# Last spectra reloaded in two parts and by tile pairs, four buffers for the first transform's results, four gate products in wide PSUM pairs, and a new written order

## The chip, the cores and the metric

The kernel runs on one core of a Trainium2 chip. Its time is device microseconds (us) of one execution. Before the change it is 236.85 us, the median of 3 runs, which lie between 234.69 and 237.14 us. One execution was recorded by the hardware profiler. It took 238.2 us, of which the profile's span, from the first instruction to the last, is 236.4 us; 1.8 us lie around the span. All positions below are microseconds from the start of that span.

## The reference

```python
def reference(A_u, A_A_re, ..., A_log_dt, A_Dskip, B_x, B_w_gate, B_w_up, B_w_down):
    x = A_u                                  # (1, 2048, 512)
    xn = layernorm(x)
    # branch A: a state-space convolution, 128 complex modes for each of 512 channels
    K[d, l] = real(sum_n C[d,n] * exp(dt[d] * A[d,n] * l) * dt[d] * B[d,n])
    y = irfft(rfft(pad(xn)) * rfft(pad(K)))[:2048] + xn * Dskip
    # branch B: a gated feed-forward layer, 512 -> 1792 -> 512
    z = (sigmoid(xn @ w_gate) * (xn @ w_up)) @ w_down
    return x + y + z
```

## The kernel before

The convolution is done by a Fourier transform in two stages, written as small matrix products on TensorE (PE). The 2048 rows of the normalised input are 16 tiles of 128 rows.

**First transform.** For two tiles at a time, `fx2` (L694) writes two PSUM pairs (a pair is 128x1024 fp32, two banks). Each is copied to SBUF by a `pl.copy` (its instruction stands at L285 when it runs on ScalarE (ACT), at L283 on VectorE (DVE)) into one of two buffers `zs` of 2 KB for each partition, and stored from there to DRAM as `z_scr` (256 KB each).

**Per-unit stage.** There are 16 units: two halves of the channels p (0, 1) and eight groups u of frequencies. Each reloads its part of `z_scr`, runs a second transform (L890, "M2"), takes swapped copies (by DMA for p=0, by VectorE at L903 for p=1), forms the kernel's spectrum from `kT` and constants E (L912, "KE", 1.09 us), multiplies the two on VectorE (L917, L921), transforms back (L934, "V", 16 matmuls), evacuates the pair (L285, into one of two `vs` buffers) and stores 256 KB to `v_scr` (L939).

**Kernel generation.** Before a half can run, its `kT` is needed. It comes from four rounds c = 0 to 3 (two for each half): powers on VectorE (L733 to L739) and squares, two blocks of 64 small matmuls each (L818, "K"), evacuations on ScalarE (L285, 128x656), 64 selection matmuls (L838, "SEL"), and an evacuation into `kT` (128x768 form of L285) with a one-row sum (L849). Round c=3 is the last; all eight units p=1 wait for it.

**Last transform.** `v_scr` has one DRAM tile for each half p. All units of a half must be stored before its tile can be read. 16 loads (L980) of 256 KB bring it into `vall`, one for each half and each t of 8 pairs of output tiles: the eight of p=0 and half of those of p=1 from SyncE's queue (SP), the rest (t odd, p=1) from ScalarE's queue. `s2_mm` (L991, L993, "Y t") multiplies one pair of tiles; every Y reads both halves, p=0 and p=1, in one access. `final` (L1006) adds the feed-forward result and x and stores.

**Feed-forward.** In four groups of 512 rows and 14 slices k of 128 features: a gate product G (L1023, 0.86 us in one PSUM bank), a sigmoid (L1032, 128x512), an up product U (L1038, 0.86 us), for some of the 56 (listed in `UEV`) a copy of U to SBUF by ScalarE (L1049), and the product of both on VectorE (L1053). Then four down products D of 14 matmuls each (L1076, 3.03 us), evacuated at L285 ("glu_sb<-bank"). The last group runs beside the last transform.

**What sets the order.** Every operation is added to a plan by its number, with its buffers to be taken and freed. A list written out by hand, `ORDER` (L202 to L243), gives the order in which all of them are issued. Each engine, and each DMA queue, runs its operations strictly in that order, so an instruction that waits holds up all that stands behind it on its engine. `ON_DVE` (L200) lists the copies that run on VectorE in place of ScalarE. The plan's costs and due times (`PF1`, `PSIG` and so on) do not decide anything here, because the list is given.

**Names that the steps below touch.** `zs` pool (L338), `v_scr` (L406), the seeds of the kernel generation and its fill `hm` (L768 to L773), `vall` and its loads (L973 to L981), `s2_mm` (L986), the gate and its sigmoid (L1019 to L1054).

The load of one t before the change, and how Y reads it:

```python
vall = at(0, [NP, 8, 2, 2, DW])              # half, t, j, r, 256 channels
v_v = v_scr[p][:]....rearrange("(p j i) d -> p j i d", j=2, i=NT)
dma("SP" if p == 0 or t % 2 == 0 else "ACT", vall[:, p, t], v_v[:, :, 2*t:2*t+2, :], ...)(256 * KB)
T.matmul(o[64*j:64*j+64, :], s2[:, r, :], vall[:, ps, t, j, r, :], ...)   # ps: both halves
```

Of the kernel before, what the change touches and what calls it, by code (L numbers as in the profile page):

```python
# [10 lines left out]
BF = mybir.dt.bfloat16  # L11
F32 = mybir.dt.float32
I32 = mybir.dt.int32
ACT = mybir.ActivationFunctionType
# [6 lines left out]
D = 512  # L21
# [21 lines left out]
LATE = (3,)  # L43
PF1 = 58.63
# [131 lines left out]
def _consts():  # L176
# [22 lines left out]
UEV = (0, 2, 4, 5, 9, 10, 14, 15, 16, 18, 19, 20, 23, 24, 25, 27, 28, 29, 30, 31, 32, 33, 34, 36, 37, 38, 39, 40, 41, 42, 43, 44, 47, 50, 51, 52, 54)  # L199
ON_DVE = (54, 57, 60, 84, 96, 107, 108, 110, 120, 121, 123, 167, 177, 179, 180, 182, 214, 230, 273, 308, 481, 565, 573)  # L200
ON_ACT = (0, 2)
ORDER = [  # L202
    0, 23, 22, 19, 1, 33, 24, 25, 32, 34, 9, 2, 3, 35, 26, 89, 36, 42, 43, 45, 44, 37, 39, 21, 18, 27, 46, 47, 48, 12,
    10, 5, 28, 38, 29, 4, 13, 102, 87, 90, 88, 6, 49, 7, 40, 30, 20, 31, 607, 41, 92, 91, 101, 8, 54, 100, 648, 649,
    14, 17, 11, 618, 619, 53, 93, 96, 623, 55, 624, 97, 653, 608, 638, 609, 50, 639, 56, 625, 643, 57, 658, 115, 626,
    644, 95, 595, 141, 596, 94, 98, 654, 659, 613, 628, 597, 142, 614, 51, 58, 144, 143, 629, 598, 640, 599, 641, 627,
    103, 52, 60, 642, 601, 131, 602, 59, 104, 603, 61, 663, 620, 655, 621, 664, 645, 660, 600, 630, 62, 134, 631, 214,
    99, 145, 132, 15, 105, 661, 656, 657, 622, 64, 662, 665, 610, 632, 666, 667, 106, 63, 646, 65, 611, 66, 615, 616,
    116, 107, 108, 67, 633, 635, 636, 634, 650, 68, 617, 612, 647, 70, 651, 69, 72, 133, 604, 146, 684, 716, 605, 71,
    167, 606, 686, 147, 135, 148, 652, 637, 114, 687, 109, 215, 73, 685, 668, 74, 670, 168, 216, 169, 113, 75, 110, 76,  # L210
    149, 117, 118, 170, 688, 77, 171, 676, 79, 151, 172, 217, 78, 717, 80, 119, 82, 81, 669, 111, 150, 173, 671, 152,
    678, 112, 704, 83, 679, 153, 154, 744, 705, 745, 123, 120, 84, 155, 677, 174, 749, 136, 139, 706, 694, 746, 707,
    750, 695, 218, 85, 86, 177, 180, 724, 725, 747, 734, 739, 185, 748, 121, 186, 187, 178, 708, 189, 190, 735, 137,
    122, 179, 219, 188, 175, 689, 714, 715, 820, 161, 736, 193, 194, 718, 140, 138, 821, 740, 737, 16, 195, 182, 738,
    726, 731, 690, 164, 732, 729, 183, 730, 165, 124, 751, 162, 699, 700, 752, 196, 709, 719, 163, 156, 197, 701, 220,
    191, 727, 159, 728, 710, 720, 702, 184, 733, 157, 198, 703, 199, 753, 200, 192, 691, 711, 712, 201, 696, 697, 698,
    202, 203, 204, 713, 782, 160, 358, 158, 205, 206, 176, 692, 181, 126, 741, 721, 742, 722, 780, 802, 723, 129, 125,
    130, 127, 128, 743, 207, 209, 221, 693, 208, 803, 832, 754, 224, 232, 233, 236, 237, 210, 833, 234, 449, 359, 235,
    240, 225, 227, 226, 211, 229, 755, 222, 241, 242, 756, 231, 212, 213, 450, 360, 243, 261, 244, 757, 238, 762, 764,
    672, 245, 248, 239, 361, 763, 246, 247, 250, 451, 230, 362, 262, 249, 263, 264, 765, 223, 758, 766, 830, 831, 434,  # L220
    363, 389, 364, 228, 781, 785, 770, 800, 435, 251, 265, 252, 801, 436, 253, 771, 266, 267, 834, 268, 374, 452, 254,
    256, 271, 257, 273, 255, 805, 806, 783, 804, 792, 258, 279, 276, 308, 280, 784, 259, 810, 811, 790, 439, 456, 272,
    277, 283, 260, 284, 438, 281, 791, 457, 680, 455, 453, 366, 269, 285, 786, 793, 458, 812, 375, 365, 454, 282, 794,
    309, 815, 367, 287, 278, 368, 816, 441, 459, 286, 460, 817, 818, 369, 396, 437, 426, 310, 370, 288, 825, 795, 461,
    819, 376, 464, 377, 813, 274, 796, 390, 289, 814, 822, 772, 290, 391, 462, 773, 442, 443, 823, 291, 827, 419, 440,
    444, 393, 394, 392, 775, 776, 275, 826, 292, 824, 293, 445, 294, 774, 397, 835, 371, 398, 836, 797, 372, 777, 381,
    395, 379, 471, 297, 798, 778, 295, 380, 463, 399, 799, 779, 270, 420, 465, 787, 807, 828, 837, 856, 400, 421, 298,
    296, 311, 466, 788, 382, 299, 789, 312, 383, 808, 300, 401, 918, 472, 838, 402, 857, 473, 301, 378, 422, 373, 303,
    302, 318, 304, 861, 317, 809, 384, 829, 385, 313, 423, 839, 326, 314, 321, 322, 470, 467, 327, 330, 331, 386, 404,
    539, 387, 405, 411, 425, 328, 329, 406, 319, 334, 840, 427, 862, 407, 409, 388, 863, 315, 335, 316, 408, 469, 424,  # L230
    428, 320, 336, 446, 531, 324, 447, 864, 563, 323, 540, 919, 325, 865, 337, 483, 842, 858, 338, 403, 412, 429, 848,
    339, 430, 342, 541, 413, 859, 431, 305, 850, 340, 341, 343, 332, 344, 345, 346, 347, 333, 432, 306, 307, 348, 350,
    349, 351, 468, 433, 410, 479, 480, 352, 414, 415, 481, 843, 841, 851, 357, 166, 564, 916, 896, 353, 448, 474, 527,
    860, 543, 551, 917, 354, 484, 565, 485, 849, 544, 878, 542, 475, 545, 416, 476, 417, 898, 567, 515, 477, 482, 486,
    487, 566, 546, 876, 899, 877, 528, 879, 529, 880, 530, 547, 568, 921, 866, 569, 478, 926, 507, 922, 552, 553, 503,
    418, 519, 488, 883, 532, 888, 920, 554, 489, 897, 533, 867, 548, 549, 504, 881, 508, 534, 570, 571, 535, 505, 889,
    509, 520, 521, 490, 491, 906, 907, 572, 492, 882, 493, 506, 356, 587, 550, 573, 884, 886, 887, 510, 900, 911, 511,
    908, 516, 536, 913, 555, 591, 517, 583, 574, 495, 579, 581, 885, 890, 518, 522, 523, 556, 537, 909, 557, 912, 512,
    901, 538, 585, 496, 891, 513, 524, 914, 902, 497, 558, 559, 494, 498, 499, 560, 903, 514, 923, 525, 904, 924, 561,
    575, 925, 576, 868, 892, 355, 593, 526, 589, 562, 500, 910, 915, 871, 893, 501, 869, 873, 905, 502, 584, 870, 872,  # L240
    592, 577, 844, 578, 894, 895, 580, 586, 874, 594, 875, 927, 930, 759, 588, 760, 761, 931, 928, 767, 938, 673, 934,
    929, 932, 590, 582, 933, 674, 675, 853, 768, 769, 852, 854, 845, 846, 939, 855, 681, 847, 682, 683, 935, 940, 941,
    936, 937, 942, 943, 944, 945]  # L243
# [72 lines left out]
def kernel(  # L316
# [21 lines left out]
    pl = _Plan(dict(s=NS, gu=NGU, hT=NHT, zs=2, zx=2, xx=3, es=3, kb=2, pp=2, pq=2, vs=2, ot=3, tg=2, us=2, sq=2))  # L338
# [8 lines left out]
    def two(slot):  # L347
        return pairs[slot.idx][:]
# [57 lines left out]
    v_scr = [dram.tile([NG, 128, DW], BF, name="v_scr%d" % p) for p in range(NP)]  # L406
# [228 lines left out]
    cur_op = pl.add("DVE", 1.25, f_w0, [q5], PR)  # L635
# [50 lines left out]
    for i0 in range(0, NT, 2):  # L686
# [10 lines left out]
        for r, sl in enumerate(sls):  # L697
            i, zsl = i0 + r, _Slot("zs")
            zs = lambda zsl=zsl: at(OFF["zs"] + zsl.idx * 2 * KB, [2, D])
            ev = pl.copy(nc, 0.90, lambda zs=zs: zs().rearrange("p j d -> p (j d)"), lambda sl=sl: two(sl),  # L700
                         [fx_mm[-1]], PF1, acq=[zsl], rel=[sl])
            fx_st.append(dma("SP", z_scr[:].rearrange("s (j i) d -> s j i d", j=2)[:, :, i, :], zs, deps=[ev], prio=PF1,
                             rel=[zsl])(256 * KB))
# [41 lines left out]
    for c in range(4):  # L745
# [22 lines left out]
        hm = pl.add("POOL", 0.3, f_hm, hdep + [cur_op], PC)  # L768
        seeds = {}
        for dst, src in ((1, 0), (7, 1), (6, 2), (8, 3), (16, 8), (27, 9), (32, 10), (40, 11)):  # L770
            seeds[dst] = pl.copy(nc, 0.31, H[:, :, dst, :, :].rearrange("p r c h -> p c r h"),
                                 W[c // 2][:, src, :, ws].rearrange("p c (r h) -> p c r h", h=2), [W_op[src], cur_op] + hdep, PC)
# [100 lines left out]
    v_st = [[], []]  # L873
    for p in range(NP):
        dsl = slice(DW * p, DW * p + DW)
        for u in range(NU // 2):
# [62 lines left out]
            v_st[p].append(dma("SP", v_scr[p][4 * u:4 * u + 4, :, :].rearrange("g q d -> q g d"),  # L939
# [32 lines left out]
    vp_op = []  # L972
    vall = at(0, [NP, 8, 2, 2, DW])  # L973
    vps = [[vall[:, p, t] for t in range(8)] for p in range(NP)]
    for t in range(8):
        lds = []
        for p in range(NP):
            v_v = v_scr[p][:].rearrange("g q d -> (g q) d").rearrange("(p j i) d -> p j i d", j=2, i=NT)
            lds.append(dma("SP" if p == 0 or t % 2 == 0 else "ACT", vps[p][t], v_v[:, :, 2 * t:2 * t + 2, :],
                           deps=v_st[p] + table_free, prio=60 + 0.01 * t if p == 0 else 20 + 0.01 * t, pkt=1024, hv=0.9)(256 * KB))  # L980
        vp_op.append(lds)  # L981
# [183 lines left out]
```

## Time and profile before

| | |
|---|---|
| median of 3 runs | 236.85 us (234.69 to 237.14) |
| profiled execution, span | 238.2 us, 236.4 us |
| PE busy | 220.5 us, 93% of the span, 2092 matmuls |
| PE loading weights (PEld, beside PE) | 112.3 us, 47% |
| VectorE (DVE) busy | 205.9 us, 87% |
| ScalarE (ACT) busy | 175.4 us, 74% |
| GpSimd (POOL) busy | 19.4 us, 8% |
| mean granted TensorE clock | 0.986 |
| bytes moved by DMA | 41.36 MB, 175 GB/s |
| last V ends, last store of `v_scr` issued, landed | 207.9, 209.07, 212.86 us |
| first Y, last matmul, end of span | 220.02, 233.34, 236.4 us |

How to read it: busy times are sums over instructions, with overlaps of one engine taken once. A row of the chain of waits gives a start, a length and what the end was waiting for at that time. "issue" is time in which an engine waited for nothing that the profile shows. The granted clock is the share of full speed that TensorE was allowed in a window. In a row such as `big<-pair`, `big` is the one large SBUF tile, `pair` and `bank` are PSUM.

### The profile page before, as it was taken

What the parts mean: (1) busy time and instruction counts of PE and PEld (TensorE: products, weight loads), DVE (VectorE), ACT (ScalarE), POOL (GpSimd) and SP (SyncE); (2) the same over time, 40 slices, a digit from 0 to 9 for tenths busy, and PEclk for the clock granted to TensorE, in tenths of its full rate; (3) what the DMA queues carried; (4) which work ended last, traced back from release to release, by engine and by line L of the source; (5) the groups of instructions that cost most, each with busy time, mean ns of one, the idle gap of its engine ahead of it and who ended that gap; (6) DMA issues with size and microseconds to landing.
All of it is one profiled execution on the core that took longest, in us unless ns stands there. A gap on an engine that the chain in (4) does not pass through costs nothing.

```text
span 236.4 us, 5411 instructions
## 1 busy us (share of the span) xinstructions
PE 220.5 (93%) x2092; PEld 112.3 (47%) x2120; DVE 205.9 (87%) x456; ACT 175.4 (74%) x284; POOL 19.4 (8%) x42
## 2 busy tenths in 40 slices
PE   7959999999899999999999999999699999997794
PEld 2434454444344364446545474456364455543352
DVE  3799999999979999999999998998679989960474
ACT  5499999999799977677999988773558897840000
POOL 1212030042000000120000000004210000000000
PEclk9999999999999999999999999999889999999799
DMA  6996299054525683089746471735638988646455
GB/s 186 367 369 238 89 225 341 16 176 90 133 87 158 192 232 95 0 173 206 220 137 166 119 215 38 202 108 165 167 106 171 303 233 249 193 121 215 129 190 177
DMA packets 46203, 41.36 MB, mean 175 GB/s; under 512 B 9057, under 2 KB 40162, under 8 KB 46178
## 3 DMA queue, kind: packets, MB, share of 16 engines
q1 hardware_dynamic: 44082, 38.33, 54.0%
q0 software_dynamic: 864, 1.57, 4.5%
q10 hardware_dynamic: 1232, 1.11, 1.7%
q8 instruction: 16, 0.26, 0.5%
q14 instruction: 9, 0.07, 0.1%
HBM read 25.28 MB, written 12.06 MB: 158 GB/s over the span
## 4 chain that ended last, share of the span: by engine, by line
PE 51%; DVE 14%; ACT 14%; DMA 13%; issue 4%; SPq 2%; ACTq 0%; DVEq 0%
PE bank L1076 13%; PE bank L1038 9%; PE bank L1023 9%; PE pair L912 6%; DMA v_scr<-big 5%; PE pair L818 5%; ACT big L285 4%; PE pair L934 4%; ACT big L662 3%; DMA big<-in_A_par_dram 3%; ACT big L668 2%; DVE big L609 2%; DMA big<-v_scr 2%; SPq L416 2%; DMA z_scr<-big 2%
## 5 line engine op out<-in xcount | busy, mean ns | idle before, releaser
L285 ACT ACTIVATE big<-pair 128x1024 bf16<-128x1024 f32 (+2 forms) x73 | 70.7, 986 | 18.4 <-PE pair L818 5.5
L1023 PE MATMUL bank<-xnT,wg_sb 128*128 128x512 bf16 (+1 forms) x224 | 53.8, 375 | 3.1 <-ACT xnT L572 1.3
L1038 PE MATMUL bank<-xnT,wu_sb 128*128 128x512 bf16 x215 | 53.1, 380 | 0.9 <-issue 0.3
L1076 PE MATMUL bank<-wd_sb,hT_sb 128*128 128x512 bf16 (+1 forms) x232 | 50.3, 367 | 0.3
L1023 PEld LDWEIGHTS <-wg_sb 128*128 128x128 bf16 x236 | 22.4, 99 | 28.2 <-issue 6.8
L1032 ACT ACTIVATE hT_sb<-bank 128x512 bf16<-128x512 f32 x56 | 33.1, 614 | 2.7 <-PE bank L1023 2.7
L1076 PEld LDWEIGHTS <-hT_sb 128*128 128x128 bf16 x238 | 22.4, 98 | 25.8 <-issue 2.5
L1038 PEld LDWEIGHTS <-wu_sb 128*128 128x128 bf16 x224 | 20.8, 98 | 25.2 <-issue 3.3
L733 DVE TENSOR_TENSOR big<-big 128x1024 bf16<-128x1024 bf16 (+4 forms) x40 | 25.7, 642 | 0.8 <-ACT big L285 0.5
L734 DVE TENSOR_TENSOR big<-big 128x1024 bf16<-128x1024 bf16 (+4 forms) x40 | 25.6, 641 | 0.0
L1049 ACT ACTIVATE us_sb<-bank 128x512 bf16<-128x512 f32 x37 | 22.6, 614 | 0.8 <-PE bank L1038 0.5
L917 DVE TENSOR_TENSOR big<-big 128x2048 bf16<-128x2048 bf16 x16 | 19.4, 1217 | 1.5 <-PE pair L934 1.1
L912 PE MATMUL pair<-big 128*128 128x256 bf16 x160 | 19.9, 274 | 0.6 <-ACT big L285 0.5
L912 PEld LDWEIGHTS <-big 128*128 128x128 bf16 x160 | 15.7, 99 | 5.9 <-issue 1.6
L738 DVE TENSOR_TENSOR big<-big 128x512 bf16<-128x512 bf16 (+4 forms) x40 | 16.8, 420 | 0.3
L786 ACT ACTIVATE sq_sb<-big 128x256 bf16<-128x256 bf16 (+2 forms) x20 | 12.8, 638 | 5.8 <-DVE big L739 3.1
L739 DVE TENSOR_TENSOR big<-big 128x512 bf16<-128x512 bf16 (+4 forms) x40 | 16.7, 416 | 0.0
L1053 DVE TENSOR_TENSOR hT_sb<-hT_sb,us_sb 128x512 bf16<-128x512 bf16 x37 | 15.2, 415 | 0.5 <-ACT us_sb L1049 0.5
L903 DVE COPY big<-big 32x1024 bf16<-32x1024 bf16 x32 | 13.4, 419 | 0.6
L1006 DVE TENSOR_TENSOR big<-pair,glu_sb 128x1024 bf16<-128x1024 f32 x4 | 4.8, 1221 | 10.2 <-PE pair L991 10.2
L1053 DVE TENSOR_TENSOR hT_sb<-hT_sb,bank 128x512 bf16<-128x512 bf16 x19 | 12.9, 681 | 0.6 <-PE bank L1038 0.3
L934 PE MATMUL pair<-big 64*64 64x512 bf16 (+1 forms) x256 | 13.1, 327 | 0.1
(104 smaller groups left out, 242.4 us busy)
## 6 DMA issues: line engine op xcount, KB each, us to landing
big<-c_E SPq DMA_DIRECT2D x16, 320.0 KB, 4.3
z_scr<-big SPq DMA_DIRECT2D x16, 256.0 KB, 2.6
big<-z_scr SPq DMA_DIRECT2D x16, 256.0 KB, 3.8
v_scr<-big SPq DMA_DIRECT2D x16, 256.0 KB, 3.4
big<-v_scr SPq DMA_DIRECT2D x12, 256.0 KB, 5.1
big<-in_A_u_dram SPq DMA_DIRECT2D x4, 512.0 KB, 6.8
big<-big SPq DMA_DIRECT2D x32, 64.0 KB, 3.2
wu_sb<-in_B_w_up_dram SPq DMA_DIRECT2D x2, 896.0 KB, 9.2
```

Of the source, the lines that this page charges most:

```text
L285: nc.scalar.activation(out=get(out), in_=get(in_), func=ACT.Identity)
L733: V.tensor_tensor(out=wide(outp), in0=wide(lo), in1=mre, op=ALU.mult)
L734: V.tensor_tensor(out=wide(tb()), in0=wide(lo), in1=mim, op=ALU.mult)
L912: T.matmul(two(sk)[:, o:o + DW], es()[:, g, kt, :], kT[p][:, kt, :], start=kt in (0, NKT - 1), stop=kt >= NKT - 2)
L917: V.tensor_tensor(out=pp().rearrange("p q h m -> p (q h) m"), in0=xx().rearrange("p q h m -> p (q h) m"), in1=kb()[:, 0:2 * DW].unsqueeze( ...
L934: T.matmul(two(sv)[o:o + 64, DW * (2 * g + y):2 * DW * (g + 1)], mab[b:b + 64, 2 * u + g, q, :], pq()[b:b + 64, q, ch] if y else pp()[b:b ...
L1023: T.matmul(bank(sl)[:, c0:c1], w[:, kt, k * 128:(k + 1) * 128], xnT[:, grp, kt, c0:c1], start=(kt == 0), stop=(kt == KT - 1))
L1032: S.activation(out=hT_sb[:, hs.idx, k % 2, :], in_=bank(sl), func=ACT.Sigmoid)
L1038: T.matmul(bank(sl), wu_sb[:, kt, k * 128:(k + 1) * 128], xnT[:, grp, kt, :], start=(kt == 0), stop=(kt == KT - 1))
L1049: S.activation(out=us_sb[:, us.idx, :], in_=bank(sl), func=ACT.Identity)
L1053: V.tensor_tensor(out=h(), in0=h(), in1=us_sb[:, us.idx, :] if on else bank(sl), op=ALU.mult)
L1076: T.matmul(bank(po)[:, 0:c[1] - c[0]], hT_sb[:, hts[k // 2].idx, k % 2, jj * 128:(jj + 1) * 128], wd_sb[:, k, c[0]:c[1]], start=first and ...
```

## The change

- **Four `zs` buffers** in place of two for the first transform's copies; the two new ones lie in a part of SBUF (`kx`) that has been used before that stage.
- **`v_scr` in three DRAM tiles:** half 0 whole; half 1, units 0 to 5; half 1, units 6 and 7. `vall` is laid out with all 16 tiles of one half and j side by side, and it is loaded by pairs of t: 12 loads in place of 16, of 512 KB (half 0), 384 KB (96 partitions) and 128 KB (32 partitions), with contiguous runs of 2 KB in place of 1 KB. A load still waits for all stores of its own tile. Two of the small loads (t=2 and t=6) are issued from ScalarE's queue, all others from SyncE's.
- **Four gate products in wide pairs:** for group 0, slices 4 to 7, two neighbouring G products go into the two banks of one PSUM pair, and one 128x1024 sigmoid takes the place of two of 128x512. The product of the even slice is issued after that sigmoid.
- **The seeds and the fill of the kernel generation** depend on two early operations (`w0_op`, `qb`) in place of the last step of the power chain.
- **`UEV`** shrinks from 37 to 29 slices copied by ScalarE, and **`ON_DVE`** names other copies: among them one table cast on VectorE in place of four, five seed copies in place of nine, eight layernorm scalings in place of seven, the `kT` evacuation of c=3 and two `glu_sb` evacuations.
- **`ORDER`** is a new list for the whole kernel. Places in it that the prediction speaks of:
  - At the start, the transposes of the second tile come earlier, and a sine chain on ScalarE stands before the third tile's evacuation.
  - In round c=3, one V, one M2 and one G stand between the K matmuls and SEL, and one V and one G between SEL and the next KE. Before the change one M2 stands between K and SEL, and one M2 and gate products between SEL and the next KE.
  - The unit that is stored last is p=1, u=2 in place of u=1. Behind its V stand G k7, U k7, a small correction product and the D products j=0 and j=1 of the last group; before the change G k3, U k7, U k3, the same correction and the same two D.
  - After the last store, SyncE issues the loads of units 0 to 5 for t=0, 6, 4, then (behind Y t=1 in the list) half 0 and units 0 to 5 for t=2. All other loads stand earlier. The last transform's order is Y t=1, D part j=0, Y t=0, j=1, Y t=4, D j=2, Y t=3, t=2, then the rest.

```diff
-UEV = (0, 2, 4, 5, 9, 10, 14, ...)
-ON_DVE = (54, 57, 60, 84, 96, ...)
+UEV = (9, 10, 11, 17, 20, 21, ...)
+ON_DVE = (81, 94, 95, 96, 97, ...)
 ORDER = [
...
-    pl = _Plan(dict(s=NS, gu=NGU, hT=NHT, zs=2, zx=2, ...))
+    pl = _Plan(dict(s=NS, gu=NGU, hT=NHT, zs=4, zx=2, ...))
...
-    v_scr = [dram.tile([NG, 128, DW], BF, name="v_scr%d" % p) for p in range(NP)]
+    VPART = ((0, 0, NU // 2), (1, 0, NU // 2 - 2), (1, NU // 2 - 2, NU // 2))
+    v_scr = [dram.tile([4 * (u1 - u0), 128, DW], BF, name="v_scr%d" % n) for n, (p, u0, u1) in enumerate(VPART)]
...
-        hm = pl.add("POOL", 0.3, f_hm, hdep + [cur_op], PC)
+        hm = pl.add("POOL", 0.3, f_hm, hdep + [w0_op, qb], PC)
...
-            zs = lambda zsl=zsl: at(OFF["zs"] + zsl.idx * 2 * KB, [2, D])
+            zs = lambda zsl=zsl: at((OFF["zs"], OFF["zs"] + 2 * KB, OFF["kx"] + 4 * KB, OFF["kx"] + 6 * KB)[zsl.idx], [2, D])
...
-            v_st[p].append(dma("SP", v_scr[p][4 * u:4 * u + 4, :, :]....
+            vn = [n for n, (p_, u0, u1) in enumerate(VPART) if p_ == p and u0 <= u < u1][0]
+            vo = 4 * (u - VPART[vn][1])
+            v_st[vn].append(dma("SP", v_scr[vn][vo:vo + 4, :, :]....
...
-    vall = at(0, [NP, 8, 2, 2, DW])
-    for t in range(8):
-        lds = []
-        for p in range(NP):
-            v_v = v_scr[p][:]....
-            lds.append(dma("SP" if p == 0 or t % 2 == 0 else "ACT", vps[p][t], v_v[:, :, 2 * t:2 * t + 2, :],
-                           deps=v_st[p] + table_free, ..., pkt=1024, hv=0.9)(256 * KB))
-        vp_op.append(lds)
+    vall = at(0, [NP, 2, NT, DW])
+    for t in range(0, 8, 2):
+        lds = []
+        for n, (p, u0, u1) in enumerate(VPART):
+            v_v = v_scr[n][:]....
+            lds.append(dma("ACT" if n == 2 and t % 4 else "SP", vall[16 * u0:16 * u1, p, :, 2 * t:2 * t + 4, :], v_v[:, :, 2 * t:2 * t + 4, :],
+                           deps=v_st[n] + table_free, ..., pkt=2048, hv=0.9)(64 * KB * (u1 - u0)))
+        vl.append(lds)
+    vp_op = [vl[t // 2] for t in range(8)]
...
-            T.matmul(o[64 * j:64 * j + 64, :], s2[:, r, :], vall[:, ps, t, j, r, :], ...)
+            T.matmul(o[64 * j:64 * j + 64, :], s2[:, r, :], vall[:, ps, j, 2 * t + r, :], ...)
...
+            joint = grp == 0 and u2 in JOINT
             for k in (2 * u2, 2 * u2 + 1):
-                a, b = _Slot("gu"), _Slot("gu")
+                a, b = _Slot("s" if joint else "gu"), _Slot("gu")
+                if joint and k % 2:
+                    a = a0
...
+                def fs2(sl=a, hs=hs):
+                    S.activation(out=hT_sb[:, hs.idx, :, :].rearrange("p k n -> p (k n)"), in_=two(sl), func=ACT.Sigmoid)
+                if joint:
+                    es_ = pl.add("ACT", 0.90, fs2, [mg], PSIG, tab="sig", acq=[hs], rel=[a]) if k % 2 else None
+                else:
+                    es_ = pl.add("ACT", 0.48, fs, [mg] + evs[-1:], PSIG, tab="sig", ...)
...
+                if joint and k % 2 == 0:
+                    held = fpd, [eu, mu], tail
+                    continue
+                if joint:
+                    prods.append(pl.add("DVE", 0.33, held[0], held[1] + [es_], PPROD, **held[2]))
+                prods.append(pl.add("DVE", 0.33, fpd, [es_, eu, mu], PPROD, **tail))
```

## The prediction

> **What bounds the kernel now.** First the page's busy times and, of the 40 slices, the row of PE.
>
> ```profile
> PE 220.5 (93%) x2092; PEld 112.3 (47%) x2120; DVE 205.9 (87%) x456; ACT 175.4 (74%) x284; POOL 19.4 (8%) x42
> ...
> PE   7959999999899999999999999999699999997794
> ```
>
> PE is the fullest engine, and no engine's work shrinks: the change adds up, by the row of each operation, to the same 215.5 us on PE, 207.5 to 207.2 on DVE and 165.0 to 165.1 on ACT (issued work without overlaps). So all it can win is PE's idle time, 236.4 - 220.5 = 15.9 us, and time at a lowered clock. The second view, busy time by stretches, says where that is (us, then PE, PEld, DVE, ACT, POOL with instructions, then the granted clock):
>
> ```profile
> 17.00:59.00 42.00, 41.47 (x223) 19.20 (x226) 41.48 (x100) 41.85 (x70) 8.57 (x12) 1.00 0.56 172
> ...
> 160.00:170.00 10.00, 8.01 (x230) 5.14 (x221) 7.47 (x12) 4.85 (x8) 3.65 (x8) 0.98 0.64 178
> 170.00:180.00 10.00, 9.74 (x77) 5.29 (x78) 8.66 (x17) 6.09 (x10) 0.86 (x1) 0.85 0.55 112
> 180.00:207.00 27.00, 26.16 (x250) 14.12 (x252) 25.26 (x42) 22.41 (x29) 0.00 (x0) 1.00 0.85 241
> ...
> 210.00:220.00 10.00, 7.03 (x34) 3.03 (x34) 1.27 (x2) 0.61 (x2) 0.00 (x0) 1.00 0.59 182
> 220.00:230.00 10.00, 9.72 (x54) 4.80 (x55) 6.41 (x7) 0.00 (x0) 0.00 (x0) 0.83 0.49 159
> ```
>
> Two stretches stand out, each followed by one with a lowered clock: 160 to 170 (2.0 us idle, then 0.85) and 210 to 220 (3.0 idle, then 0.83). Third, the chain of waits names what PE waited for in both, and in a smaller one at 63:
>
> ```profile
> 57.92 4.92 DMA z_scr<-big
> 62.95 1.02 ACT big L285
> 63.97 0.49 ACT us_sb L1049
> ...
> 165.98 0.72 ACT big L285
> 166.75 0.74 PE pair L838 x50
> 167.49 1.31 issue
> 168.80 0.35 PE pair L838 x14
> ...
> 208.02 1.03 ACT big L285
> 209.07 3.79 DMA v_scr<-big
> ...
> 215.16 5.53 DMA big<-v_scr
> 220.73 0.96 PE bank L991 x3
> ```
>
> The last piece ends a PE wait that the list of waits states alone:
>
> ```profile
> PE pair L991 <- DMA big<-v_scr: 2.9, 1, 2.9
> ```
>
> **The change part by part.** The sum is made against the profiled execution, 238.2 us, 1.35 above the median of 236.85; the same difference is taken off at the end.
>
> *Four `zs` buffers: -0.9.* At 57.92 a store of `z_scr` took 4.92 us; a copy on ACT waited 1.25 us for its buffer, the two operations behind it (1.02 and 0.49) came late, and PE idled 0.86 (63.65 to 64.51). With four buffers the copy waits for the store four back, some two copies (2 us) older. Ends: -0.9, and 0 if ACT, which is 41.85 of 42 us busy until then, is as late by itself.
>
> *Round c=3: -3.1.* Between 166.2 and 170.1 PE idles 0.51 (for the evacuations after K), 1.31 (inside SEL, "issue") and 0.22. The clock then is short of full by 10 x 0.15 + 10 x 0.02 = 1.7 us. Afterwards V, M2 and G stand before SEL (0.77 + 0.34 + 0.86 = 1.97 us) and V and G behind it (1.63). The evacuation that is waited for ends 0.8 us after K, so 1.97 covers it; the `kT` copy (0.75 on ACT; on DVE 0.9, three quarters of the 1.23 of a 128x1024 copy there) and the 0.27 sum are covered by 1.63. What goes is 0.73 of waits; the 1.31 has no releaser in the profile, and since nothing else tells, half of it (0.65) is taken; with under 2 us idle the clock window goes too, 1.7. Ends: 0 (the filler is only work from elsewhere, and what follows becomes late in its place) and -3.75 (all). What is late next is the stage of the eight units p=1: PE has 38.5 us of work there and DVE 38.05, as before, so PE still sets the pace, barely.
>
> *First wait for the reload: -0.7.* Before, from the last V's end (207.91) to the landing of the last store is 4.95 us; six loads follow, and Y starts 7.15 later, at 12.1 in all, against 9.17 of other work on PE: 2.94 of wait. Afterwards G, U, the correction and two D stand behind the last V: 2 x 0.86 + 0.32 + 6.06, with the old gaps of 0.2, 8.3 (one U less, which is done earlier). Three loads of 384 KB follow the store. Y t=1 needs only t=0's, but a Y reads across both halves, and the old trace shows such reads taken for whole intervals: two loads of ScalarE's queue, issued behind one at 213.56, left at 222.22 and 223.50 only, after Y of other t. So I count all three. Two issues of 0.63 come first, and then, by the nearest row in size (E, 320 KB: 4.3 us), 4.3: Y is ready 4.95 + 5.6 = 10.55 after V and waits 2.25. The lower clock window stays (2.0 idle brought it at 170). Ends: if only the first load counts, 4.95 + 4.3 = 9.25, wait 0.95 and no clock window, -2.0 - 1.7 = -3.7; if the third takes the 5.1 us of the old loads, 11.35, wait 3.05, +0.1.
>
> *Loads for t=2: +0.3.* 512 and 384 KB are issued on SP behind Y t=1, because that Y's read is taken as above. Issue 0.6 each, landing by the E row 4.3 or by the four 512 KB loads of the input at the start (6.8): 4.9 to 7.4 us. Beside it stand four Y parts (0.45 each at full clock, up to 0.85 in a window of half clock) and one D (3.03): 4.8 to 6.4. Wait 0 to 2.6; with the window kept, 0.3. The other loads leave before the last store; those ScalarE issues stand behind its last sigmoid, where nothing waits for ScalarE.
>
> *Start: 0.* PE idles 1.34, 0.99 and 0.32 between 11.9 and 17.3, clock 1.00. Now transposes come earlier (one gap of 1.34 goes), but the third tile's copy stands behind a sine chain on ACT (17.5), and G's second part waits some 2.1 us for it in one piece. -0.6, or, if that drops the clock as at 170, +1.1; I take the middle.
>
> *Wide gate pairs, `UEV`, `ON_DVE`, dependencies, the rest of the order: 0.* Four sigmoids of 0.48 become two of 0.90 on ACT, -0.1. In groups 0 and 1 seven copies go (-3.4 on ACT; products read PSUM at 0.60 in place of 0.335, +1.9 on DVE), three casts move to ACT (+3.1; -2.0 on DVE). Both engines stay as full as the first stretch shows, so nothing covers an error: one more stall of the size of c=3's is +3.7. At best the idle left in 17 to 59, 80 to 160 and 180 to 207 (0.5, 0.9, 0.8, by the same view) goes: -2.2. The held product waits for a later sigmoid, with other products queued behind it on DVE; its cost lies inside these ends.
>
> Sum: -0.9 - 3.1 - 0.7 + 0.3 = -4.4. 238.2 - 4.4 = 233.8, and by the median's distance **232.4 us**, 1.9% less.
>
> **A rule against the rows.** The clock fell to half for 3.4 us behind only 2.0 us (c=3) and 2.9 us (reload) of idle time. The Trainium skill ("TensorE: Matmul & The Clock Gate", "What's actually happening") says the drop takes an idle window of about 3.4 us, free-running. By that rule a wait of 2.25 us would leave the clock alone, and the sum would be 1.7 lower, 230.7; the rows decide for me. It also has each DMA at about 2.0 us and bytes over 436 GB/s ("DMA: Bandwidth & Descriptors", "Anatomy of one DMA"): 1.18 MB would take 4.7 us in place of 5.6, an estimate that would make the total 0.9 lower; the old 256 KB loads took 5.1 where it gives 2.6.
>
> **Rivals.**
> *The c=3 gain is eaten (no change).* The 1.31 "issue" recurs in SEL with its window of half clock (c=3 gives 0.73 alone, 2.4 less than forecast), and the start costs its 1.1: 235.9. For: the stall has no releaser, so filler ahead of SEL need not remove it. Against: SEL at 92.95 and 111.92 has no such stall. Chance 0.20.
> *The loads wait on one another (slower).* The new layout lets the bytes of one load lie between those of another (j strides over all 16 tiles). If writes are taken for whole intervals as the Y reads were, the three late loads go one after another, at 3.4 us (the 256 KB stores' median) to 4.3 each: 10.2 to 12.9 in place of 5.6, and of the t=2 pair the second goes behind the first, 6.8 to 8.6 against 4.9 of cover in place of 0.3 of wait: +6.2 to +10.7 on the sum, 238.6 to 243.1; I take 240. It turns the result once the late loads leave SP more than 2 us apart. Against: the gate weights' pieces, also interleaved, were issued on SP without such waits. Chance 0.13.
> *A new stall before 86 (slower).* ACT and DVE are full there; the stall of 3.7 on top of the first rival gives 239.6. Chance 0.14.
> *The reload's wait nearly goes (faster still).* Its end of -3.7: 229.4. Chance 0.10.
>
> **Numbers.** The forecast has 0.43. Faster by over 1% (2.4 us, about what a measurement of this kernel tells from no change): 0.43 + 0.10 = 0.53; within 1%: 0.20; slower: 0.27. The range is 228.0 to 240.3: it leaves out the slower half of the second rival, some of the third, and the best ends together. The faster cases alone: 228 to 234.4.
>
> **What would show it.** No PE wait on the copy of `z_scr` near 60; PE over 9.5 of 10 us around SEL of c=3, and a clock of 1.00 behind it; the wait of L991 on `v_scr` near 2.2 us, a second one under 0.9 before Y t=3; late loads 0.6 apart on SP. I am wrong if "issue" inside SEL stays, if a lowered clock appears near 17, or if PE idles for ACT between 17 and 86.

## The result and the profile after

The changed kernel takes 246.81 us (median of 4 runs, 245.34 to 247.94); the kernel before took 236.56 us beside it. The ratio is 1.0433, with a 95% interval of 1.0357 to 1.0509: 10 us slower, where the forecast was 4.4 us faster. The time lies outside the range (228.0 to 240.3). The profiled execution took 246.36 us, with a span of 244.4. Here and below a ratio compares executions in the chip's faster state alone, while a median counts all.

The busy times and PE's slices of the page, to be held against those of before:

```profile
PE 222.4 (91%) x2120; PEld 112.4 (46%) x2120; DVE 205.6 (84%) x448; ACT 174.7 (71%) x282; POOL 18.6 (8%) x42
...
PE   7969999999999999999999999999999999801694
...
PEclk9997999999999999999999999999999999965598
```

The busy times of PE, VectorE and ScalarE differ by under 1%, and the dip at c=3 (a 6 in PE's row of before) is gone. All of the loss stands in the last six slices. Busy time by stretches, cut at the end of the last V, for the changed kernel (the columns are those of the stretches shown of before):

```profile
163.00:176.00 13.00, 12.91 (x264) 8.39 (x254) 11.41 (x21) 10.40 (x15) 0.62 (x2) 1.00 0.73 189
176.00:204.20 28.20, 27.69 (x270) 14.41 (x269) 27.64 (x47) 22.48 (x30) 4.38 (x9) 1.00 0.74 211
204.20:244.40 40.20, 22.69 (x121) 10.32 (x119) 12.18 (x21) 2.13 (x3) 0.00 (x0) 0.77 0.42 126
```

The same for before, cut at its own last V:

```profile
163.00:176.00 13.00, 10.95 (x237) 7.12 (x236) 9.97 (x16) 6.17 (x10) 3.58 (x9) 0.87 0.55 139
176.00:207.90 31.90, 30.91 (x313) 16.57 (x318) 29.26 (x54) 26.12 (x34) 0.81 (x1) 1.00 0.84 233
207.90:236.40 28.50, 22.17 (x127) 10.83 (x125) 12.66 (x17) 2.59 (x4) 0.00 (x0) 0.94 0.52 165
```

The last V ends 3.7 us earlier (204.2 against 207.9), and what follows it takes 40.2 us in place of 28.5: 11.7 us more, with nearly the same busy time of PE (22.7 and 22.2 us), 17.5 us of idle time in place of 6.3, and a mean clock of 0.77. The chain of waits of the changed kernel says what filled it:

```profile
203.37 0.80 PE pair L935 x16
204.17 0.02 issue
204.19 1.03 ACT big L285
205.22 0.02 issue
205.24 3.00 DMA v_scr<-big
208.24 0.02 issue
208.25 4.54 DMA big<-v_scr
212.79 0.02 issue
212.81 3.76 DMA big<-v_scr
216.57 0.02 issue
216.59 3.73 DMA big<-v_scr
220.32 0.25 issue
220.56 1.05 PE pair L994 x3
221.61 0.02 issue
221.63 0.56 SPq L417
222.19 0.04 issue
222.23 5.75 DMA big<-v_scr
227.98 0.04 issue
228.02 0.64 PE bank L994
```

The three late loads follow one another: each one's first piece is issued 0.02 us after the landing of the one before. Of the four matmuls of Y t=1 one runs behind the first load, the other three when the third has landed:

```profile
212.83 0.38 PE L994 MATMUL pair<-big 128*64 128x512 bf16 x1
220.56 1.03 PE L994 MATMUL pair<-big 128*64 128x512 bf16 x3 [7.35 <-DMA big<-v_scr]
```

The first one reads j=0: taken as one interval from half 0 to half 1, its read ends ahead of the places of t=4 and t=6 in half 1. The second reads j=1, and its interval runs over them. The two loads of t=2 are issued 0.6 us apart behind Y t=1, and the next Y part (L994, bank), which multiplies a tile of t=6, starts when they have landed. The list of waits gives both for PE, and for SyncE's queue in that stretch a wait of 7.2 us, in two pieces, on the loads themselves:

```profile
PE pair L994 <- DMA big<-v_scr: 7.4, 1, 7.4
...
PE bank L994 <- DMA big<-v_scr: 6.4, 1, 6.4
```

```profile
SPq L417 <- DMA big<-v_scr: 7.2, 2, 4.0
```

Before, PE had one wait there, of 2.9 us. So the second rival is what happened. Which cause stands behind it, and what the rest of the change is worth, the runs below tell.

### The profile page after: what moved, and what is told of

The parts are those of the page before. It is cut to its first block, busy times and chain, and to the rows that moved or that the text cites. A ratio compares the mean times of both kernels' runs of the same rounds, so it can differ in the third digit from the quotient of the medians.

```text
span 244.4 us, 5428 instructions
## 1 busy us (share of the span) xinstructions
PE 222.4 (91%) x2120; PEld 112.4 (46%) x2120; DVE 205.6 (84%) x448; ACT 174.7 (71%) x282; POOL 18.6 (8%) x42
## 4 chain that ended last, share of the span: by engine, by line
PE 80%; DMA 10%; ACT 4%; DVE 2%; SPq 1%; issue 1%; POOL 0%; DVEq 0%; ACTq 0%; POOLq 0%
PE bank L1054 18%; PE bank L1098 18%; PE bank L1030 17%; DMA big<-v_scr 7%; PE pair L913 6%; PE pair L819 4%; PE bank L523 4%; PE pair L935 3%; PE pair L891 2%; PE pair L994 2%; DMA big<-big 2%; PE pair L1030 1%; PE pair L839 1%; ACT big L285 1%; DMA v_scr<-big 1%; PE pair L695 1%
## 5 line engine op out<-in xcount | busy, mean ns | idle before, releaser
L285 ACT ACTIVATE big<-pair 128x1024 bf16<-128x1024 f32 (+2 forms) x74 | 73.1, 994 | 16.6 <-PE pair L913 3.9
L1054 PE MATMUL bank<-xnT,wu_sb 128*128 128x512 bf16 x224 | 54.9, 380 | 0.0
L1030 PE MATMUL bank<-xnT,wg_sb 128*128 128x512 bf16 (+1 forms) x220 | 52.4, 377 | 2.4 <-ACT xnT L573 2.4
L1030 PEld LDWEIGHTS <-wg_sb 128*128 128x128 bf16 x236 | 22.9, 100 | 27.7 <-issue 6.0
L1098 PEld LDWEIGHTS <-hT_sb 128*128 128x128 bf16 x238 | 22.9, 98 | 26.4 <-issue 3.2
L1042 ACT ACTIVATE hT_sb<-bank 128x512 bf16<-128x512 f32 x52 | 30.5, 618 | 1.2 <-PE bank L1030 1.1
L1069 DVE TENSOR_TENSOR hT_sb<-hT_sb,bank 128x512 bf16<-128x512 bf16 x27 | 18.0, 679 | 0.6 <-ACT big L285 0.6
L1065 ACT ACTIVATE us_sb<-bank 128x512 bf16<-128x512 f32 x29 | 17.7, 612 | 0.0
L285 ACT ACTIVATE big<-big 128x256 bf16<-128x256 bf16 x31 | 12.5, 440 | 3.3 <-PE pair L819 3.3
L904 DVE COPY big<-big 32x1024 bf16<-32x1024 bf16 x32 | 14.0, 438 | 0.5
```

What stands on the lines that cost most here:

```text
L285: nc.scalar.activation(out=get(out), in_=get(in_), func=ACT.Identity)
L1030: T.matmul(bank(sl, k % 2)[:, c0:c1], w[:, kt, k * 128:(k + 1) * 128], xnT[:, grp, kt, c0:c1], start=(kt == 0), stop=(kt == KT - 1))
L1042: S.activation(out=hT_sb[:, hs.idx, k % 2, :], in_=bank(sl), func=ACT.Sigmoid)
L1054: T.matmul(bank(sl), wu_sb[:, kt, k * 128:(k + 1) * 128], xnT[:, grp, kt, :], start=(kt == 0), stop=(kt == KT - 1))
L1065: S.activation(out=us_sb[:, us.idx, :], in_=bank(sl), func=ACT.Identity)
L1069: V.tensor_tensor(out=h(), in0=h(), in1=us_sb[:, us.idx, :] if on else bank(sl), op=ALU.mult)
```

## The experiments

**Contiguous blocks.** Two theories for the row of loads: (A) the program makes each load wait, because a piece that is strided over j is taken for its whole interval in SBUF, and so overlaps its neighbours; (B) the transfers are slow by themselves. This run changes only where the bytes lie in SBUF. The instructions of every engine stand in the same order as in the changed kernel.

```diff
-    vall = at(0, [NP, 2, NT, DW])
+    vall = at(0, [4, NP, 2, 4, DW])
...
-  vall[16 * u0:16 * u1, p, :, 2 * t:2 * t + 4, :]
+  vall[16 * u0:16 * u1, t // 2, p, :, :, :]
...
-  vall[:, ps, j, 2 * t + r, :]
+  vall[:, t // 2, ps, j, 2 * (t % 2) + r, :]
```

> The changed kernel with one edit: the reloaded spectra lie in SBUF as one contiguous block for each tile pair (both halves side by side) in place of all 16 tiles of one half and j side by side. Same 12 loads, same bytes, same packets, same queues, same order. Theory A (the late loads wait on one another because a strided piece is taken for its whole interval, writes and reads alike): the late loads leave SyncE's queue 0.6 us apart, Y t=1 waits for the t=0 loads alone, PE waits 0 to 1 us there and at no later Y; from V's end at 204.1 us, 4.1 for the last store, 4.5 for the first load, then 15 to 16.5 us to the end: about 231 us in all, 5 us under the kernel before. Theory B (the transfers are slow by themselves, for their 96 partitions, packets of 2 KB or reading what was just stored): 246 to 247 us as the changed kernel, loads still about 3.8 us apart.

Measured: 232.48 us (median of 10 runs) against 236.21 of the kernel before, ratio 0.9822 (0.9777 to 0.9867). That is 14.3 us less than the changed kernel. Its chain of waits:

```profile
204.67 3.25 DMA v_scr<-big
207.92 0.02 issue
207.93 0.56 SPq L417
208.49 0.05 issue
208.54 0.60 SPq L417
209.14 0.04 issue
209.18 7.11 DMA big<-v_scr
216.29 0.04 issue
216.33 0.64 PE pair L994 x4
```

and its waits of PE on the reloaded spectra:

```profile
PE bank L994 <- DMA big<-v_scr: 1.0, 1, 1.0
PE pair L994 <- DMA big<-v_scr: 0.5, 1, 0.5
```

The late loads leave 0.6 us apart and are in flight together; SyncE's queue has no wait on them. The third takes 7.1 us from its issue where it took 3.7 alone, but Y t=1 does not wait for it: it starts at 212.75, and all later waits sum to 1.5 us. The rest after V is 25.9 us in place of 40.2. Theory A holds, theory B falls; the size (231 expected) was 1.5 us too good.

**The halves apart.** Here the writes are contiguous, but each Y reads across both halves, past the blocks of other tile pairs.

```diff
-    vall = at(0, [NP, 2, NT, DW])
+    vall = at(0, [NP, 4, 2, 4, DW])
...
-  vall[16 * u0:16 * u1, p, :, 2 * t:2 * t + 4, :]
+  vall[16 * u0:16 * u1, p, t // 2, :, :, :]
...
-  vall[:, ps, j, 2 * t + r, :]
+  vall[:, ps, t // 2, j, 2 * (t % 2) + r, :]
```

> As the run with contiguous blocks, but with the halves apart again: each load writes one contiguous block, while every Y still reads across both halves. It takes away the overlap of the writes alone. Theory A: late loads 0.6 us apart, but Y t=1 waits for all three (PE wait 1 to 2.5 us), and the first Y part behind it waits for the loads of t=2, which leave only after Y t=1 (another 4 to 6 us): 236 to 239 us. Theory B: 246 to 247 us.

Measured: 238.64 us, ratio 1.0107 (1.0068 to 1.0145). The trace is of the longest of the ten executions, 242.91 us. Its list of waits has one on the spectra:

```profile
PE bank L994 <- DMA big<-v_scr: 6.5, 1, 6.5
```

It is the part behind Y t=1, which waits for the loads of t=2; they were issued at 217.44 and 218.04, right behind Y t=1 (216.79 to 217.43). Y t=1 itself came with 0.9 us of idle time ahead of it, less than expected: in this layout its interval runs over the later blocks of half 0 and not over the places of t=4 and t=6 in half 1. So the change has two false waits: the late loads on one another, with Y t=1 behind them (246.81 to 238.64, 8.2 us), and reads against writes of other tile pairs (238.64 to 232.48, 6.2 us). The split is not a clean one of writes and reads, since Y t=1 lost its wait for t=4 and t=6 in the first step. The wait of reads was in the prediction for the three loads, and forgotten for the Y parts that were to cover the loads of t=2.

**The new layout in the old kernel.** Only the place of the bytes in SBUF is changed, in the kernel before.

```diff
-    vall = at(0, [NP, 8, 2, 2, DW])
-    vps = [[vall[:, p, t] ...
+    vall = at(0, [NP, 2, NT, DW])
+    vps = [[vall[:, p, :, 2 * t:2 * t + 2, :] ...
...
-  vall[:, ps, t, j, r, :]
+  vall[:, ps, j, 2 * t + r, :]
```

> The kernel before with one edit: vall in the layout of the changed kernel (all 16 tiles of one half and j side by side), still 16 loads of 256 KB with runs of 1 KB. Theory A: the eight late loads of half 1 go one after another at about 3.7 us each, over both queues: 250 to 262 us. Theory B: the transfers are the same, 236 to 238 us.

Measured: 258.94 us, ratio 1.0968 (1.0895 to 1.1042), 23 us for a layout alone. Part of its chain:

```profile
216.51 2.98 DMA big<-v_scr
219.49 0.02 issue
219.50 3.07 DMA big<-v_scr
222.58 0.02 issue
222.59 3.20 DMA big<-v_scr
...
225.96 3.02 DMA big<-v_scr
...
229.00 3.15 DMA big<-v_scr
```

256 KB with runs of 1 KB, over two queues, one after another at 3.0 to 3.2 us. Neither the parts, nor runs of 2 KB, nor the new order is needed for the loss. What no run tells is which strided slices are taken so. In the trace of before the three pieces of the gate weights, strided too, were issued at 3.58, 4.06 and 7.98 us and took 8.8 to 9.9 us to land, so none waited for another. They lie in a tile of their own, `wg_sb`, while `vall` is a view of `big`; whether that makes the difference is open.

**Four buffers alone.**

```diff
-    pl = _Plan(dict(..., zs=2, ...
+    pl = _Plan(dict(..., zs=4, ...
...
-  at(OFF["zs"] + zsl.idx * 2 * KB, [2, D])
+  at((OFF["zs"], OFF["zs"] + 2 * KB, OFF["kx"] + 4 * KB, OFF["kx"] + 6 * KB)[zsl.idx], [2, D])
```

> The kernel before with four zs buffers and nothing else. The prediction's step says that the 0.86 us of PE idle at 63.65 goes and the total falls by 0.9 us (235.7). Its rival: ScalarE is as late by itself, the idle time returns with another releaser, and the total stays within 0.3 us.

Measured: 235.72 us (median of 12) against 236.21, ratio 0.995 (0.9907 to 0.9993): 1.2 us less by the ratio, between 0.2 and 2.2, and 0.5 less by the medians. In its trace PE has no gap between 55.8 and 73. The step is right in direction, and 0.9 lies inside the interval; so does the rival's 0.3, at its lower end.

**The filler of round c=3.** From here on, the kernel with contiguous blocks is the base, unless another is named. In it V and G are put back behind SEL. (A list of another length moves the line numbers by one or two: SEL is L838 before, L839 in the changed kernel and L841 here.)

```diff
-order: K, K, [evacuations], V p0u3, M2 p1u1, G g3k2, SEL, V p0u4, G g3k10, KE
+order: K, K, [evacuations], M2 p1u1, SEL, V p0u3, G g3k2, V p0u4, G g3k10, KE
```

> The kernel with contiguous blocks per tile pair (232.5 us), with the V and the G that stand between K and SEL of round c=3 put back behind SEL; one M2 stays between. Theory F (the 1.31 us of issue inside SEL is PE waiting for its next block of instructions: in the two traces with the stall, a 16 KB packet of the instruction queue is seen at 166.4 and 165.4 us and PE goes on 2.4 us later): the stall comes back, 0.5 us of wait ahead of SEL and 0.8 to 2 us inside it; with the clock window that makes 234 to 236.2 us. Rival (the filler only moved idle time; what stands behind takes it up): within 0.5 us of 232.5.

Measured: 233.85 us, ratio 0.990 (0.9832 to 0.9968), 1.4 us over the base by the medians, with intervals that overlap slightly, and just under the range of theory F (234 to 236.2). PE's rows of the timeline around SEL (here L841), with the idle time ahead of each and its releaser:

```profile
166.12 0.41 PE L893 MATMUL pair<-big,m 64*64 64x512 bf16 x4 [0.21 <-DMA big<-z_scr]
166.76 0.67 PE L841 MATMUL pair<-big,sw 128*32 128x96 bf16 x45 [0.24 <-ACT big L287]
168.40 0.40 PE L841 MATMUL pair<-big,sw 128*32 128x96 bf16 x19 [0.97 <-issue]
```

The stall without a releaser is back, 0.97 us, after 45 of the 64 matmuls; the lowered clock that theory F added is not (1.00 for the whole execution). A 16 KB packet of the instruction queue stands at 165.8 in this trace; PE goes on 2.6 us later. In the trace of before the packet stands at 166.4 and PE goes on at 168.80 (2.4, after 1.31 us of stall), with four buffers at 165.4 and 167.90 (2.5, after 2.15 us). So three traces fit one account: K and SEL are 192 small matmuls with as many weight loads, 384 instructions in some 3.5 us, a packet holds some 265, if that queue serves PE (4240 instructions of PE, 16 packets), and PE runs out of instructions until the next block can be used. The base has its packet at 165.0, and the V, M2 and G ahead of SEL pass the time: its whole stretch 163 to 176 has 0.2 us of idle time. That the stall goes with the filler and returns without it is seen in these traces; that the stall is the instruction block's is argued from these times, since no run changed the block itself. The Trainium skill ("Runtime: NRT & Kernel Launch", "Instruction fetch mechanics") has refills in blocks of 16 KiB, 256 instructions, and calls the cost of a boundary mostly hidden. If the account is right, a boundary cost 0.97, 1.31 and 2.15 us of idle PE in these three traces.

**The same filler in the kernel before.**

```diff
-order: K, K, [evacuations], M2 p1u0, SEL, products p0u3, copy of M2, ..., V p0u3
+order: K, K, [evacuations], products p0u3, V p0u3, M2 p1u0, copy of M2, SEL, ...
```

> The kernel before with one move: one V (p=0, u=3) with its products and its evacuation stands ahead of the M2 and SEL of round c=3, in place of behind SEL. Theory F: PE's 2.04 us of idle around SEL fall to 0.5 to 0.9 and the half clock behind it goes (1.7 us): 233 to 234 us against 236.2. Rival (the stage of the units p=1 is paced by VectorE): idle falls, but comes back before 207, 235.5 to 236.5 us.

Measured: 236.03 us, ratio 1.001 (0.9967 to 1.0053). In its trace the idle time around SEL is 0.69 in place of 2.04 and the clock stays at 1.00, as expected, but the median gains nothing, as the rival has it. The rival's mechanism is not shown, though: the trace is of the fastest of the ten executions (234.99 us), its last V ends at 206.0, 1.9 us ahead of the trace of before, and between 176 and 206 PE is idle for 1.26 us (before: 0.99) and VectorE busy for 28.9 of 30 (before: 27.5). Eight of the ten executions have a mean clock of 0.993 or less, so they still hold a stretch at half clock, and no trace tells where. So the -3.1 of this step was not to be had for itself, and why is open. In the new order the filler is worth about 1.4.

**The start.** The copy of the third tile goes ahead of the sine chain on ScalarE.

```diff
-order on ACT: L573 (tile 1), L621, L624 to L627, L573 (tile 3)
+order on ACT: L573 (tile 1), L573 (tile 3), L621, L624 to L627
```

> The kernel with contiguous blocks per tile pair, with the third tile's copy (L573) put ahead of the sine chain on ScalarE. Theory: the 2.4 us wait of G's second part falls to about 1.3, and the half clock that follows it in part of the executions goes: 230.5 to 231.7 us. Rival (the sine chain feeds the power chain on VectorE, which is full until 86): no gain or up to 1 us slower, 232.5 to 233.5 us.

Measured: 232.16 us, ratio 0.9818 (0.9754 to 0.9881): between the two ranges, and not to be told from the base. The trace is of the longest of the four executions (235.44 us). In it G's second part no longer waits, but the wait has only moved: right behind these matmuls of G PE idles 2.16 us, until 20.24, for a sigmoid of ScalarE (L1044), and a stretch at half clock follows. PE also waits 1.6 us near 146 and 1.56 at the reload.

**The order of the last transform.** D j=2 goes ahead of the Y parts that wait, the loads of t=2 ahead of Y t=1.

```diff
-order: Y t1, loads t2, Y j0, Y t0, Y j1, Y t4, D j2
+order: loads t2, Y t1, Y t0, D j2, Y j0, Y j1, Y t4
```

> The kernel with contiguous blocks per tile pair, with D j=2 of the last group ahead of the first Y parts that wait (behind Y t=1 and t=0), and the two loads of t=2 issued ahead of Y t=1. Theory: the two waits of 0.97 and 0.51 us on reloaded spectra go: 231 us. Rival (the stores and the final sums set the end): 232 to 233 us.

Measured: 234.25 us, ratio 0.9888 (0.9795 to 0.9982). No gain; the median lies above both ranges (231, and 232 to 233). From the last V to the end it takes 26.1 us, the base 25.9, as the rival has it; PE now waits 1.0 us on spectra at t=3 and 1.07 on a final sum of VectorE. The profiled execution (234.96 us) was longer for another reason, which the waits between 130 and 151 show, for PE and VectorE:

```profile
PE bank L1100 <- ACT hT_sb L1044: 2.7, 1, 2.7
```

```profile
DVE big L920 <- DMA big<-big: 3.0, 1, 3.0
```

The chain there: the swap copies of p=0, u=0 took 6.38 us (6.78 in the run with the halves apart, 4.31 in the changed kernel), VectorE waited 3.0 us with them at the head of its queue, behind it the power chain, the squares and a sigmoid on ScalarE, and for that sigmoid PE. The changed kernel and the base show 0.4 and 0.3 us of this wait of VectorE, for the same instructions.

**A later product.** The waiting product is issued after six other operations of VectorE, 2.1 us.

```diff
-order on DVE: pa p0u0, 5 of the power chain and others, pb p0u0, power 12, powers 17 and 12
+order on DVE: 5 of the power chain and others, power 12, pa p0u0, pb p0u0, powers 17 and 12
```

> The kernel with contiguous blocks per tile pair, with the first product of p=0, u=0 on VectorE (L918) and the one behind it issued after six operations of the power chain in place of ahead of them (2.1 us of other work). Theory: in part of the executions the swap copies it waits for land 6.4 to 6.8 us after issue in place of 4.3, VectorE then idles 3.0 to 3.5 us near 142 and PE 1.6 to 3.2 near 146; with 2.1 us of work ahead of it, the longer executions (234 to 235 us) become rare and the median falls by 0.5 to 1.5 us, to 231 to 232 us. Rival (the lateness returns at the V that follows): 232 to 233 us with the same spread.

Measured: 232.34 us, six executions within 232.05 and 233.06, ratio 0.9873 (0.9826 to 0.9921). Neither VectorE nor PE waits between 130 and 152. The median is that of the base; the spread is 1.0 us where the base's ten had 4.1 (230.5 to 234.7). The expected spread came, the expected median (231 to 232) did not: the long executions are gone, but four of the base's ten were faster than the fastest of these six, and what the best ones lost is not known.

**Both moves.**

> Both moves together: the later product, and the third tile's copy (L573) ahead of the sine chain. Theory: the two add up, 230.5 to 231.5 us. Rival (the sine chain's delay of 1 us is passed on by VectorE): no better than the later product alone.

Measured: 231.62 us (230.1 to 232.7) against 236.09, ratio 0.9827 (0.9772 to 0.9881). It lies just above the expected range. It beats the kernel before by 4.5 us by the medians and is the best that was run, but its leads over the contiguous blocks alone and over the later product alone (232.34) lie inside the intervals, so that the two add up is not shown. Here too the wait at the start has moved: PE idles 2.00 us, until 18.84, for the sigmoid.

## Why the prediction was wrong

*The cause, in one sentence:* the late loads wait on one another, the second rival, to which the prediction gave 0.13, and its working chose against it on a single row (the interleaved pieces of the gate weights, issued without waits, a reading that is right and did not carry over).

- **First wait for the reload, -0.7: the step that failed.** It had the three loads issued 0.63 us apart and the third landing 5.6 us after the store. They went one after another (4.54, 3.76, 3.73), 12.1 us. PE waited 7.4 us, not 2.25. The trace of before had the evidence: Y's reads were taken for whole intervals there. The prediction used that for the reads of Y and not for the writes of the loads, though the new layout strides both.
- **Loads for t=2, +0.3: failed too,** by the other half of the same rule. The two loads, one for each half, did leave 0.6 us apart and landed 6.4 us after the first issue, inside the 4.9 to 7.4 that was given. But the Y parts that were to cover them waited for them: 6.4 us.
- **The rival's price, 238.6 to 243.1, was too low** for that reason and for the clock: its row of loads (10.2 to 12.9 us) was right. Against the contiguous blocks the three late matmuls of Y t=1 start 7.2 us later after V, and the later waits are 4.9 us longer. That leaves 2.2 of the 14.3 us by which the traces differ behind V, and PE's busy time there, at the lowered clock, is 2.8 us longer.
- **Four buffers, -0.9:** right in direction by the run with nothing else (-1.2, between -0.2 and -2.2; -0.5 by the medians).
- **Round c=3, -3.1:** the waits and the lowered clock went as described, and V ended 3.7 us earlier in the traces, near the 4.0 of the two steps. But its size is not confirmed: 1.4 in the new order, 0 in the old. The profiled execution of before had two stretches of half clock (mean clock 0.986) and was 2 us longer than the median of the 29 later runs (236.2). 21 of those have a mean clock of 0.992 or more, which is one such stretch or none, so the sum counted lowered clock that most executions do not have.
- **Start, 0, with +1.1 if the clock drops:** G's second part waited 2.4 us in one piece (2.1 expected), and the clock behind it dropped in the trace of the changed kernel and not in that of the contiguous blocks.
- **Wide pairs, `UEV`, `ON_DVE`, the order elsewhere, 0:** no run took these apart. The new order has one thin place, the swap copies near 140: in the profiled execution with the last transform reordered PE waited 2.7 us behind them.
- **The rule on the clock:** the rows came nearer than the rule, and neither is the whole of it (last section). The other figure that is quoted, for a load's time, is given in its section of the Trainium skill ("DMA: Bandwidth & Descriptors", "Anatomy of one DMA") for transfers on GpSimd's path. The loads here leave from SyncE, and one of 384 KB alone took 3.7 to 3.8 us, where an estimate by that figure is 2.9.

With the layout mended, the kernel takes 232.5 us against the 232.4 forecast. That agreement is partly luck: the reload came out better (1.5 us of waits and full clock in place of 2.55 us and half clock), the rest worse.

## What to carry to other kernels

Ask of every strided slice, for writes and reads, what interval the program's ordering takes it for, and look in the trace of before for a wait that only such an interval explains; if there is one, lay the buffer out so that what is loaded together and read together is one block. A gain in issue or packet size is nothing against a row of transfers that no longer overlap. And take the sum against several executions' times, not against one whose clock was low.

## What the runs showed of the hardware

- **The clock after a gap of 2.4 us depends on where the gap falls.** The wait of G at the start was 2.37 us in the changed kernel and 2.42 with contiguous blocks. These are the stretches behind it, of the first and then of the second kernel:

```profile
16.80:20.20 3.40, 3.39 (x17) 1.98 (x17) 3.37 (x6) 3.29 (x4) 0.67 (x1) 0.64 1.04 391
```

```profile
16.80:20.20 3.40, 2.72 (x19) 1.85 (x19) 3.37 (x6) 3.37 (x5) 0.09 (x1) 1.00 1.04 391
```

  0.64 and 1.00 for gaps of one length (the second gap ends at 17.48, inside its stretch). The clock's records in the traces tell them apart. Its lowered stretches last 3.41 us or whole multiples of it, up to 17.07 in the tail of the changed kernel. Cut into windows of 3.41 us that fit these edges, the gap of the changed kernel lies in one window (14.34 to 17.75, 2.37 us idle); the other gap is cut at 15.70 into 0.64 and 1.78 us. In the twelve traces all 18 windows at full clock in which PE idled for 2.0 us or more were followed by half clock, and none with under 1.8 us was; in between, one was (1.83, round c=3 of before) and two were not (1.88, 1.93). The Trainium skill ("TensorE: Matmul & The Clock Gate", "What's actually happening") has a free-running window of about 3.4 us, and that agrees; if its "idle window" is read as one that is idle throughout, it does not fit, since 2.0 us was enough here.
- **Transfers together are slower for each, and better in all.** Three loads of 384 KB took 12.1 us one after another (208.25 to 220.32) and, five loads in flight, 8.4 us from the first issue (207.93) to the landing of the third (216.29).
